# One scan of logarithms in place of two scans of products, in a fused decayed attention and feed-forward kernel

## The chip, the cores and the metric

One NeuronCore of a Trainium2 chip runs the whole program. The metric is device time in microseconds (us). Names: TensorE is PE (its weight loads are PEld), VectorE is DVE, ScalarE is ACT, GpSimd is POOL, and SP is the queue that issues nearly all DMAs.

## The reference

Four batches of eight heads, 768 steps, head size 48. Each step multiplies a 48 x 48 complex state by a complex decay per row, adds the outer product of k and v to its real part, and reads it with q. The result feeds a feed-forward layer (384 to 2048 to 384) with g = h * sigmoid(1.702 h).

```python
mag = np.sqrt(a_re * a_re + a_im * a_im)
scale = np.minimum(mag, 0.999) / (mag + 1e-06)
a_re_n, a_im_n = (a_re * scale, a_im * scale)
...
for t in range(S):
    ar, ai = (a_re_n[:, :, t, :, None], a_im_n[:, :, t, :, None])
    new_re = ar * S_re - ai * S_im
    new_im = ar * S_im + ai * S_re
    kv = np.einsum('bhd,bhe->bhde', k[:, :, t], v[:, :, t])
    S_re, S_im = (new_re + kv, new_im)
    y[:, :, t] = np.einsum('bhd,bhde->bhe', q[:, :, t], S_re)
```

The inputs: a_re is uniform in 0.85 to 0.95, a_im is normal with a spread of 0.1.

## The kernel before

The 4 x 768 steps are twelve units of 256 steps (`prepare(u)`, `attend(u)`); the first unit is prepared in two halves of 128. A unit is prepared in the layout rows x steps, three groups of rows side by side (NR = 3), so that 256 steps are tiles of 128 x 768 elements, and a half is 128 x 384.

`prepare_part` turns the decays into factors. Per step it needs the magnitude min(mag, 0.999) / (1 + 1e-6 / mag) and the angle of the complex number. Squares of re and im (`sqr`, `sqi`) are added (`sum`); Ln and Exp with scale 0.5 give mag (`root`); the angle is twice arctan(im / (re + mag)), with a maximum-and-add on DVE (`den`), a reciprocal by Ln and Exp (`logd`), a product (`ratio`) and Arctan (`atan`). A second reciprocal (`logc`) and a line on it (`w`) make the small correction. A backward scan of products (`sp`) gives the decay from each step to the end of the unit, which scales k; a forward scan of products (`qm`) that starts at the reciprocal of the unit's whole decay (`edge`) gives its inverse, which scales q. A third scan sums angles (`theta`); rounding, absolute value and two Sin give cosine and sine, with which q and k are turned. Ten DMAs per unit (`remap`; for halves too) bring q and k to the layout of heads x steps.

`attend` multiplies q and k to scores (p_ps), masks them on DVE (pm), multiplies them and the running state with v (x_ps), copies the result as x, and updates the state (kz_ps, st). `moe(n)` takes blocks of one or two units through the hidden layer (h_ps, Silu on ACT) and the output layer (o_ps). The weights come as 64-bit words and are made into fp32 on ACT and DVE (`convert`); from the third block on they are split in two parts (`split`), three matmuls each. `inspect`, `sign` and `decide` look at the inputs' ranges; if one is out of bounds a slow general branch runs. `clear` zeroes the tile qkh1 in pieces on POOL.

ACT's functions stand in table sets: LOGS (Ln, Exp), TRIG (Arctan, and Sin for the first unit), SILU (Silu, Sin). Where the next activation needs another set, a table load is put ahead of it.

All this is recorded as operations in a `Plan`; a stored order (`ORDER`, a packed list of numbers) says in which order they are issued, and `OTHER` names those that run in their second form on another engine. Each engine takes its instructions strictly in that order.

Of the kernel before, what the change touches and what calls it, by code (L numbers as in the profile page):

```python
# [106 lines left out]
}  # L107
ORDER = (
    "08jve0000A00jUK0A&DD08s!_0D}O808{{l0962n09F8p09OEr09gP509XKB0E++v0Eqw#09pWF09yc$00sbz0FVG&0A2u!0AT=)0AK)-0Am1-"
    "0Ac|U0FwZ}00#hQ0I2|y0G9w{0BHaM0BQgX0A~PZ0Bitj0F(f20Ga^^0B!*Z0F?l50SW+{0B``70C50w0TBS40GR-u0CE8m0G$930CWJK0D%CQ"  # L110
    "0H6R30CfQq0CoVP0Tcjt0HFY*0C)fr01*JB0HpyH00aQC0T}?Q0Hy&J0H*+X0Sf@L0JH!I0D1uz0H^?~0JQ)K0T=+b0IUHT022Uv0IdMH0DJ)-"
    "02u&%03!f?0Ji}k01g1I02BbP0J#8v0k#1f0Vn{v03HCq0J{O00I&eO0KovU0Vx2z0Kx#i0LTEt0K@>v0UZFv0V)8-0UiMi0UQ7%0LlQz0Du7@"
    "03`s_0VM#-0NMa10V4q`0U`hz0M!5|0M-B-02Kf?0N?-|02Tox0N4QB0k{Cy0L%a#0W1K{0NDT+0k;4x03QI)0O9}`0NVf{03iS<0WJX00Ve?A"
    "0MP+003rb105|~S05SmG0l5I*0VV;u0WbjP0lNV&0WkpN0lxvf0WtvQ0W$%;0L=lw05bsX04V{!04@M30PFxO05t&80W<*a0ObHI0W|>V0Sy5*"
    "051SK0O|ng05AYK0mA_605JgX05k!`0P+FB05$<Q0mcEs0S*B306YQ20Mh}-06_po0Pq3M0m%Um0YL#d0YU*o0Pz7j0Ym}M0XG4r0Y?Bk0XqQo"
    "0X+f8080Tp0Yw4J0QdpQ0Z0M<0Zjo(0Qmqt0Y(5m0nh<H0ZIWs06zfq0Qvy?06+mw0iXd(073!M0agG<0QLb_0Z#x!07L;$07wB$07U^<0YCuv"
    "0a*Y^0hRzv0RI8e07?K&0Z{<{0RaF`0n`D^0n-5d0nGvc0o4Hg0sjHk0RRC~0s#S20oMW80a^f00aOA40ipq10s{d80bK!A0t5mG0bT)O0ha;>"
    "0onoy0cipU0oeiD0b>FV0o(y!0uKRb0tEqO0v7=T0crvY0dE2f0;U050b~LV0t*5d0uTXo0R#aB0c!zn0R{pR0ucff0uuq>0bl{>0rUaj0cHW-"
    "0vQ1Z0cQcS0viEg0qFv#0ki>Z0jdFU0vZCX0pS650;mD%0pbC50vrOV0v!St0c`<r0;&Ps0dfKB0hs}$0eS+f0v`dI0u=#s0w4mg0v-YG0qg>?"
    "0;~cd0rdgz0ek`D0ptR-0p$Vk0rmlV0h|Hx0wV!<0eu3p0qp`L0<{7n0p<aQ0<!^k0h<Ay0wn?R0jvVJ0rvu~0f7OX0=fZt0p|j*0rLT{0fzyf"  # L120
    "0=5Bw0=WYF0=EJ90e%7|0j>hS0=xl(0x$w60r>*J0x<#l0=ohG0x|+T0sH}f0fGX-0{j7l0sR8Q0w@AA0{sDn0>lFX0jL5g0f_;K0yF|D0yY9G"
    "0yhFZ0{#Ll0xbcd0yqLL0gVFx0zLvY0yzRd0xtoh0y+Xl0?z{g0g3{?0y_f*0=)r?0|o-e0gM7i0zd(e0>}c!0!RWu0|5fb0geJf0!acx0>T1H"
    "0z?8#0>uH40!0E#0|NsG0#gFZ0i^>30|^3B0#^dc0}2BO0?Y#q0?h(V0g(d_0!{&v0$l=F0}cZV0#pJ|0#ySH0h0rm0$c)F0h9t(0$~Fb0$KwR"
    "0$u@?0jC2M0?-2x0#E|k0$Ty80$&3b0%ihY0$>7B0?q<t0%!vh0~i8h1DXR80%rpm0@?!61DOLC0~-Qm0&4@C0~!My0%-%B0^0&?0&xQ!0^9>0"
    "0jmOP1DyhG0@MQ110VyU0^I?v0^b861ET_N0^kFr0^S3j1Em6R1EvDg1E&KY0&fGV0&)W)0(AqR0j~n#1FQn(1D^ub0^$PJ0&@c60_6hN0`CK%"
    "0(%1R1E>Pn1E~V>1FiwF0(t^=10(|E0(1iB0(b)Q0(=5@1F-`20_XyL1F{110_g(k0)GLs0_y_y0_*{`10@1}273bc1FHgs1MCAP0{8>70__5M"
    "27Cjw0`vp011AE20{H_d11<uD27LoB27Uti1FZsr0)YeV1Fr+M0)qqY0)_*(27dyF0*M1K0*(TT12G1G1GWN)27v?f13Cha1Gxf=1G)l?27&^U"
    "0`3Fv10w_Q0+|E21Mvg91NH;*12h9E12O|D12Y3V12qHp11kcM12zLJ0*wQ_0+9nZ0+Ivt0+<6W13U(U0+a@X12_Y{0-6Iq1Hc140+j-m13m-#"
    "1NZ|u1Nj5{1HJ;61HS^B0-XY!13&_v1O5X+0-ysz1N8$#1ONh`14IM-289Hb1N{U428IHm14agi1O)^F14RO&1O@`514jc+14#o)14{;o15W~^"
    "14ssm1P2C+1Hl7R1OWre15g7@1Iq*i15E=_1PKI}1Iz<i1HuE%1eOE{15yTy15^f#16T%)0;L1i1JDD`1H%K+16l)C1H=Rh1egR1162f>17ZVP"  # L130
    "1Pum`1P%lP1eycV16KoF1JeV~17rq|1Plg{17HJP1P=pV178E+1Jnb>29X2T1K|Xp1e^oL1IGlL1L6Z?17!rD1P}w`29g8F17QRa29pD417-vg"
    "1QP?;18f7;1fv9@1f&F_1g8Vp18xK41f2us18M_k1gQp;1IYxQ19k&%1Lp>n1KI|b1f>IQ18D@_1f~OU1giwD19$`#18W0u1g`_=19t=E19AiD"
    "19JqZ2A2bL2ABk@2AKpO1KR|!1m6S}19=171hNC_1Kk8519}7@2ATta1M37A1R?~p2Ac%n2Al(X19b!51gr$%1hE7o1mXjH1Q-UL1A+u41g!&p"
    "1APXb1SSNu1QZ6J1hxZ#1S<oB1K$MY1SbQ31BC;G1SkaK1Q`Ui1R4Y+1S|%i1n30h1RDe#2B8Gz1iA*I1SteH1RVsv1i1r<1iJ+11ndMh1iS?4"
    "1T6!K2BQOp1S$j`1UCdO1ULhX1UUpR1TX~Z1Th5e1TqBc1nmQj1UmzV1B(PY1C9oy1n>r>1BnBV1oQ+v1TzHh1T+Nl1h)jZ1Cj%f1Ca#x1Cs>t"
    "1%?Dd1C#{w1VIEw1C<2$1o;F#1WW`&1VjUt1Vsc(2Bri@1V{w+1W5!<1oi~`1XTq51WpF01&9Wy1U>{$1iu9S1V04G1o{Nj1pfs61WE&!1Xl$B"
    "1px(z1W*Nu1XBc21&Ri#1X2WF1p@@h1&aj01q1{@1ib{o2C4+g1&ju(1XcuC1&##*1&{<;1XKkD1j__r1YHDL1&;(<1i}Q)1k41(1kD7*1&svH"
    "1l0sw1jPhm1(pQR1jYnl1knV?1(5}m1(yb_1(gMo1YQQM1(OAs2Cf8T1Zf1;1)2q)1la`F1Z4!$1Y-pd1ZoDa1ZxGE2CxMY1lR_#1ZD-C1ZM=("
    "1qKD11rh{v2C@Yc2D1gA2DAmC1=|E@1Z)MP1Z@SR1r`Mq1a1V{2DJqj1)c=k1)T*41snw21sDW%2DSur1aAcy2Db&=1r-Ev1)>F}1aSm-1*Zk2"
# [878 lines left out]
```

## Time and profile before

| | |
|---|---|
| median of 3 runs | 564.99 us (564.89 to 565.46) |
| profiled execution, first to last instruction (span) | 563.2 us |
| PE busy | 532.4 us, 95% |
| PE weight loads | 442.2 us, 79% |
| DVE busy | 447.3 us, 79% |
| ACT busy | 313.2 us, 56%, of it 61 table loads with 78.3 us |
| POOL busy | 24.5 us, 4% |
| granted TensorE clock | 1.00 throughout |

The profile gives no time of that execution but its span; the median of the runs is some 1.8 us longer. PE starts late and is then busy to the end: its row in 40 slices of 14 us reads 0, 2, 8 and then 9 to the last. DVE and ACT are most taken in the first third.

### The profile page before, as it was taken

The page shows a single profiled execution, that of the slowest core. Times are in us where ns is not written, and L with a number is a line of the kernel's source. Part 1 is how long each engine was busy: PE and PEld are TensorE (multiplying, and loading weights), DVE is VectorE, ACT ScalarE, POOL GpSimd, SP SyncE. Part 2 cuts the span into 40 slices and gives each one's busy share as a digit, 9 for nine tenths or more (in the row PEclk, how much of TensorE's full clock was granted, in tenths as well). Part 3 has the DMA queues.
Part 4 walks back from the last instruction along what each step waited for, and adds up shares of the span by engine and source line. Part 5 has one row for each costly group of instructions (what it writes and reads, how often), then busy time and mean ns, then how long its engine had stood idle before and what let it go on. Part 6 is the DMA issues. An engine that isn't in the chain of part 4 may idle for free.

```text
span 563.2 us, 14767 instructions
## 1 busy us (share of the span) xinstructions
PE 532.4 (95%) x6236; PEld 442.2 (79%) x6236; DVE 447.3 (79%) x820; ACT 313.2 (56%) x460; POOL 24.5 (4%) x86
## 2 busy tenths in 40 slices
...
GB/s 307 199 194 359 181 381 76 222 102 221 72 146 119 128 148 101 113 150 122 136 180 75 167 128 210 45 227 94 103 138 56 203 122 87 51 52 70 29 61 110
DMA packets 30902, 80.06 MB, mean 142 GB/s; under 512 B 4208, under 2 KB 7024, under 8 KB 30832
## 3 DMA queue, kind: packets, MB, share of 16 engines
...
HBM read 55.44 MB, written 4.72 MB: 107 GB/s over the span
## 4 chain that ended last, share of the span: by engine, by line
PE 92%; DVE 5%; ACT 1%; DMA 1%; issue 0%; DVEq 0%
PE o_ps L646 37%; PE h_ps L613 37%; PE x_ps L532 7%; PE p_ps L507 5%; PE kz_ps L563 4%; PE kz_ps L557 3%; DVE s L427 1%; DVE qk L271 1%; DMA ri<-in_a_dram 1%; DVE pm L511 1%; DVE s L271 0%; DVE qr L271 0%; DVE s L409 0%; DVE s L393 0%; DVE valA L298 0%
## 5 line engine op out<-in xcount | busy, mean ns | idle before, releaser
L626 ACT ACTIVATE g<-h_ps 128x512 f32<-128x512 f32 x80 | 46.3, 596 | 120.8 <-PE h_ps L613 79.7
L613 PE MATMUL h_ps<-xhi,hiA 128*128 128x512 f32 x240 | 95.9, 400 | 0.0
L646 PE MATMUL o_ps<-gh,hiU 128*128 128x512 f32 x240 | 95.5, 398 | 0.0
L646 PE MATMUL o_ps<-gl,hiU 128*128 128x512 f32 x240 | 93.7, 390 | 0.0
L613 PE MATMUL h_ps<-xhi,loA 128*128 128x512 f32 x240 | 93.6, 390 | 0.0
L646 PE MATMUL o_ps<-gh,loU 128*128 128x512 f32 x240 | 93.5, 390 | 0.0
L613 PE MATMUL h_ps<-xlo,hiA 128*128 128x512 f32 x240 | 93.5, 389 | 0.0
L843 ACT ACT_TABLE_LOAD x61 | 78.3, 1283 | 1.9 <-PEq L1006 0.8
L630 DVE CAST gh<-g 128x512 fp32r<-128x512 f32 x70 | 29.4, 421 | 42.5 <-PE o_ps L646 25.5
L632 DVE TENSOR_TENSOR gl<-g,gh 128x512 fp32r<-128x512 f32 x80 | 54.5, 684 | 3.0 <-ACT gh L629 1.3
L646 PEld LDWEIGHTS o_ps<-gl,hiU 128*128 128x128 f32 x240 | 45.0, 188 | 10.0 <-DVE gl L632 0.4
L613 PEld LDWEIGHTS h_ps<-xhi,loA 128*128 128x128 f32 x240 | 45.0, 188 | 9.6
L680 DVE TENSOR_REDUCE fit<-raw_w 128x1 f32<-128x256 f32 x96 | 38.1, 413 | 18.0 <-DMA raw_w<-in_w_out_dram 17.7
L646 PEld LDWEIGHTS o_ps<-gh,hiU 128*128 128x128 f32 x240 | 45.1, 188 | 9.2 <-issue 0.4
L646 PEld LDWEIGHTS o_ps<-gh,loU 128*128 128x128 f32 x240 | 45.1, 188 | 8.7
L613 PEld LDWEIGHTS h_ps<-xlo,hiA 128*128 128x128 f32 x240 | 45.1, 188 | 8.5
L613 PEld LDWEIGHTS h_ps<-xhi,hiA 128*128 128x128 f32 x240 | 45.1, 188 | 8.5
L511 DVE TENSOR_TENSOR pm<-p_ps,mask 128x512 f32<-128x512 f32 x48 | 32.8, 682 | 17.2 <-PE p_ps L507 13.9
L566 ACT ACTIVATE kt<-kz_ps 128x224 f32<-128x224 f32 x66 | 23.3, 353 | 40.5 <-PE kz_ps L563 29.9
L271 DVE TENSOR_TENSOR qk<-qk,s 128x768 f32<-128x768 f32 (+1 forms) x52 | 45.7, 889 | 0.0
L646 PE MATMUL o_ps<-g,valU 128*128 128x256 f32 x192 | 45.3, 380 | 0.0
L613 PE MATMUL h_ps<-x,valA 128*128 128x256 f32 x192 | 45.0, 381 | 0.0
...
## 6 DMA issues: line engine op xcount, KB each, us to landing
...
```

What stands on the lines that cost most here:

```text
L271: add(en, t, rank, lambda: e.tensor_tensor(out=out, in0=a, in1=b, op=alu), **kw)
L507: mm(p_ps[to : to + QL, j, lo:L], lhsT=at(h, 1, c)[:, lo : lo + QL], rhs=at(h, 0, c)[:, lo:L], start=True, stop=True)
L511: add("DVE", d_t(CW), rk(4 * c + hh), lambda hh=hh: dve.tensor_tensor(out=pm[hh], in0=p_ps, in1=mask, op=ALU.mult), r=["P"], w=[f"pm{hh}"])
L532: mm(x_ps[32 * j : 32 * j + 32, r, :], lhsT=lt, rhs=rt, start=n == 0, stop=n == len(steps) - 1)
L566: one = ("ACT", a_t(2 * KD) - 0.12, lambda e=e: act(out=kt[0][:, 2 * e : 2 * e + 2, :], in_=k_ps, func=AF.Copy))
L613: mm(h_ps[hb][:, hs], lhsT=ww[:, r * T + f * P : r * T + (f + 1) * P], rhs=x[:, r, :], start=r + k == 0, stop=r == NR - 1 and k == len(ter ...
L626: add("ACT", a_t(N) - 0.15, rk(i + f / 2), lambda hb=hb, hs=hs: act(out=g32[hb][:, hs], in_=h_ps[hb][:, hs], func=AF.Silu, scale=SLOPE), r ...
L630: two = ("DVE", d_t(N, 2), lambda hb=hb, hs=hs: dve.tensor_copy(out=high.g(hb)[:, hs], in_=g32[hb][:, hs]))
L632: add("DVE", d_t(N), rk(i + f / 2), lambda hb=hb, hs=hs: dve.tensor_tensor(out=glo[hb][:, hs], in0=g32[hb][:, hs], in1=high.g(hb)[:, hs].b ...
L646: mm(o_ps[m][:, 0:N], lhsT=y[:, f * DM + m * P : f * DM + (m + 1) * P], rhs=x[:, hs], start=i == 0 and f == 0 and k == 0, stop=i == NP - 1 ...
L680: add("DVE", d_t(CK), rk + 2, lambda x=x, op=op: dve.tensor_reduce(out=f_w[:, x, n : n + 1], in_=weights.looked_at()[:, :, 1], op=op, axis ...
L843: nc.scalar.preload_act_table_set(o[5])
```

## The change

The two scans of products become one backward scan that sums logarithms (ADD of min(0.5 Ln(mag^2), Ln 0.999), SUBTRACT of Ln(1 + 1e-6 / mag)), started at LIFT = 14. ACT takes Exp of it for k, and Exp of its negative for q; the common factor e^14 cancels. The clamp, the reciprocal and the forward scan (`edge`, `scan_qm`) are gone, and so are `root`'s Exp and the DVE line `w`. The angle is arctan(im / re) itself: `den` is gone, and `logd` takes Ln and Exp of re. For that the check of the inputs is another: re must be at least |im| (`extent` in place of `sign`, with twice the loads and reduces), and late units get a reduce of |im| beside that of re. The turn in `theta` is 2 pi, not pi. The order and the list of second forms are new.

```diff
-        square("sqi", u, i, rk("sqi"), d, i_, r=ks("im"), w=k_den, tab=opening)
-        both("sum", u, i, rk("sum"), m, m, d, ALU.add, r=k_den, w=k_mag)
+        square("sqi", u, i, rk("sqi"), c, i_, r=ks("im"), w=k_rec, tab=opening)
+        both("sum", u, i, rk("sum"), m, m, c, ALU.add, r=k_rec, w=k_mag)
+        add("ACT", a_t(C), rk("logd"), lambda: act(out=d, in_=r_, func=AF.Ln, bias=b_tiny), r=ks("re"), w=k_den, tab=LOGS, grp=u or None)
+        add("ACT", a_t(C) - 0.1, rk("logd"), lambda: act(out=d, in_=d, func=AF.Exp, scale=-1.0), w=k_den, tab=LOGS, grp=u or None)
         add("ACT", a_t(C), rk("root"), lambda: act(out=m, in_=m, func=AF.Ln, bias=b_tiny), w=k_mag, tab=LOGS, grp=u or None)
-        add("ACT", a_t(C) - 0.1, rk("root"), lambda: act(out=m, in_=m, func=AF.Exp, scale=0.5), w=k_mag, tab=LOGS, grp=u or None)
-        add("DVE", d_t(C) + 0.18 * C / (NR * T), rk("den"), lambda: dve.scalar_tensor_tensor(
-            out=d, in0=r_, scalar=0.0, in1=m, op0=ALU.max, op1=ALU.add
-        ), r=ks("re") + k_mag, w=k_den)
...
+            add("DVE", d_t(NR * T), rk("low"), lambda: dve.tensor_reduce(
+                out=f_i[:, u - LATE : u - LATE + 1], in_=i_, op=ALU.max, axis=AX.XY, apply_absolute_value=True
+            ), r=["im.0", "im.1"], w=["fi"])
+        add("ACT", a_t(C) - 0.1, rk("logc"), lambda: act(out=c, in_=m, func=AF.Exp, scale=-0.5), r=k_mag, w=k_rec, tab=LOGS, grp=u or None)
+        add("ACT", a_t(C), rk("logc"), lambda: act(out=c, in_=c, func=AF.Ln, scale=1e-6, bias=ones), w=k_rec, tab=LOGS, grp=u or None)
...
         add("DVE", w_t(C), rk("z"), lambda: dve.tensor_scalar(
-            out=m, in0=m, scalar1=0.999, scalar2=None, op0=ALU.min
+            out=m, in0=m, scalar1=0.5, scalar2=LOG_MAX, op0=ALU.mult, op1=ALU.min
         ), w=k_mag)
...
-                    initial=1.0, op0=ALU.mult, op1=ALU.mult,
+                    initial=LIFT, op0=ALU.add, op1=ALU.subtract,
...
-        def edge():
-            dve.tensor_scalar(out=rc, in0=w(sp)[:, :, 0], scalar1=A_MIN, scalar2=None, op0=ALU.max)
-            dve.reciprocal(out=rc, in_=rc)
...
-        add("DVE", NR * (s_t(n) + 0.055), rk("qm"), scan_qm, r=k_mag + k_rec + [f"rc{u % 2}"], w=k_qm)
+        add("ACT", a_t(C) - 0.1, rk("qm"), lambda: act(out=w(qm), in_=w(sp, 1, 1), func=AF.Exp, scale=-1.0), r=k_sp, w=k_qm, tab=LOGS, grp=u or None)
+        add("ACT", a_t(C) - 0.1, rk("sp"), lambda: act(out=w(sp, 0, 1), in_=w(sp, 0, 1), func=AF.Exp), w=k_sp, tab=LOGS, grp=u or None)
+        add("POOL", 0.13, rk("qm"), lambda: pool.tensor_scalar(
+            out=fa, in0=w(sp)[:, :, 0], scalar1=math.exp(-LIFT), scalar2=None, op0=ALU.mult
+        ), r=k_sp, w=[f"fa{u}.{i}"])
...
-        add("POOL", 0.45, 14 + 0.5 * n, lambda: pool.memset(part, 0.0), r=["rc0"], w=[f"H1.{c}.{x}" for c in range(2) for x in range(2)])
+        add("POOL", 0.45, 14 + 0.5 * n, lambda: pool.memset(part, 0.0), r=["s3.0"], w=[f"H1.{c}.{x}" for c in range(2) for x in range(2)])
```

The first place where the order differs is POOL at the program's start, behind the masks. In the rows, s is a tile of the preparation, fit the table of checks, qkh_76 the tile that is zeroed in pieces. Before:

```order
L386 MEMSET s_80 128x3
L382 MEMSET s_82 128x3
L386 MEMSET s_80 128x3
L405 COPY fit<-s_83 128x3
L382 MEMSET s_82 128x3
L721 MEMSET qkh_76 128x513 x2
L405 COPY fit<-s_83 128x3
L721 MEMSET qkh_76 128x513
L458 COPY qr<-fit 128x3
L458 COPY qk<-fit 128x3
L721 MEMSET qkh_76 128x513
L386 MEMSET s_82 128x3
```

And of the change:

```order
L385 MEMSET s_82 128x3
L389 MEMSET s_80 128x3
L385 MEMSET s_82 128x3
L715 MEMSET qkh_76 128x513
L389 MEMSET s_80 128x3
L715 MEMSET qkh_76 128x513 x2
L404 TENSOR_SCALAR fit<-s_83 128x3
L715 MEMSET qkh_76 128x513 x5
L404 TENSOR_SCALAR fit<-s_83 128x3
L450 COPY qr<-fit 128x3
L450 COPY qk<-fit 128x3
```

Three pieces of zeroing now stand ahead of the first copy of the edge (L404, which waits for the decay's Exp), and five in a row behind it; before they were spread over the opening and beyond it.

The second place is DVE in the opening, where the decay's scans of the second half and the angles stand; s_83 is the sum or product of decays, s_85 the angle. Before:

```order
L393 SCALAR_TENSOR_TENSOR s_83<-s_80,s_82 128x129 x3
L271 TENSOR_TENSOR s_81<-ri,s_81 128x3x128
L401 TENSOR_SCALAR small<-s_83 128x3
L402 RECIPROCAL small<-small 128x3
L393 SCALAR_TENSOR_TENSOR s_83<-s_80,s_82 128x129 x3
L427 SCALAR_TENSOR_TENSOR s_85<-small,s_81 128x128 x3
L409 SCALAR_TENSOR_TENSOR s_84<-s_80,small,s_82 128x128 x3
L437 SCALAR_TENSOR_TENSOR s_85<-s_85,s_81 128x3x128
L271 TENSOR_TENSOR qk<-qk,s_83 128x3x128
L271 TENSOR_TENSOR qk<-qk,s_84 128x3x128
L440 TENSOR_SCALAR small<-s_85 128x3
```

And of the change:

```order
L429 SCALAR_TENSOR_TENSOR s_85<-s_85,s_81 128x3x128
L277 TENSOR_TENSOR s_81<-ri,s_81 128x3x128
L436 SCALAR_TENSOR_TENSOR s_80<-s_85 128x3x128
L277 TENSOR_TENSOR qk<-qk,s_84 128x3x128
L386 TENSOR_SCALAR s_80<-s_80 128x3x128
L277 TENSOR_TENSOR qk<-qk,s_83 128x3x128
L432 TENSOR_SCALAR small<-s_85 128x3
L396 SCALAR_TENSOR_TENSOR s_83<-s_80,s_82 128x129 x3
L277 TENSOR_TENSOR qr<-qk,s_80 128x3x128 x2
L419 SCALAR_TENSOR_TENSOR s_85<-small,s_81 128x128 x3
```

The clamp (L401), the reciprocal (L402) and the scans of L409 have gone; two tensor-scalar instructions, L386 (halving and minimum) and L432 (the angle's carry), stand around the second product.

The third place is ACT ahead of the copies of x, from the rounding of the second half's angle (L434 before, L426 now) on. Before:

```order
L434 ACTIVATE s_81<-s_85 128x3x128
L254 ACTIVATE s_82<-ri 128x3x256
L443 ACTIVATE s_80<-s_85 128x3x128
L254 ACTIVATE s_81<-ri 128x3x256
L446 ACTIVATE s_80<-s_80,small 128x3x128
L447 ACTIVATE s_85<-s_85 128x3x128
L843 ACT_TABLE_LOAD
L368 ACTIVATE s_82<-s_82,small 128x3x256
L294 ACTIVATE valA_238<-raw_74 128x768
L369 ACTIVATE s_82<-s_82 128x3x256
```

And of the change, the first rows from one Sin on:

```order
L439 ACTIVATE s_85<-s_85 128x3x128
L837 ACT_TABLE_LOAD
L402 ACTIVATE s_84<-s_83 128x3x128
L426 ACTIVATE s_81<-s_85 128x3x128
L403 ACTIVATE s_83<-s_83 128x387
L837 ACT_TABLE_LOAD
L438 ACTIVATE s_80<-s_80,small 128x3x128
L300 ACTIVATE valU_150<-raw_73 128x768
L300 ACTIVATE valA_166<-raw_74 128x768
L439 ACTIVATE s_85<-s_85 128x3x128
L260 ACTIVATE s_82<-ri 128x3x256
L837 ACT_TABLE_LOAD
```

Before, one table load stands between the second half's rounding and the logarithms of the next unit (L368; L373 of the change). Now two stand there, and a third just ahead of the rounding, since the two Exp of the decay's sum come between one Sin and the next.

## Rows read from the trace of the kernel before

**Rows 1.** The page: busy time and share of each engine; the chain that ended last, by engine.

```profile
PE 532.4 (95%) x6236; PEld 442.2 (79%) x6236; DVE 447.3 (79%) x820; ACT 313.2 (56%) x460; POOL 24.5 (4%) x86
...
PE 92%; DVE 5%; ACT 1%; DMA 1%; issue 0%; DVEq 0%
```

**Rows 2.** Windows: stretch, its length, each engine's busy time (instructions); clock, DMA share, GB/s.

```profile
0.00:43.63 43.63, 17.02 (x326) 13.02 (x327) 39.81 (x82) 34.28 (x56) 9.99 (x30) 1.00 0.68 239
43.63:100.00 56.37, 56.37 (x645) 48.55 (x645) 55.46 (x90) 51.39 (x75) 4.04 (x11) 1.00 0.77 242
100.00:460.00 360.00, 359.90 (x4456) 299.43 (x4455) 305.49 (x545) 211.73 (x300) 10.44 (x45) 1.00 0.53 137
460.00:563.23 103.23, 99.13 (x813) 81.24 (x812) 46.51 (x106) 15.81 (x31) 0.00 (x0) 1.00 0.21 66
...
151.40:233.80 82.40, 82.35 (x1071) 68.63 (x1064) 72.88 (x125) 58.18 (x79) 3.00 (x13) 1.00 0.51 126
```

**Rows 3.** Waits of PE: line waited for, us in total, times, longest.

```profile
PE h_ps L454 <- DVE small L440: 24.6, 1, 24.6
```

**Rows 4.** Timeline before the first hidden matmul: start, length, engine, line, operation.

```profile
40.74 0.69 DVE L511 TENSOR_TENSOR pm<-p_ps,mask 128x512 f32<-128x512 f32 x1 [0.25 <-PE p_ps L507]
...
43.07 0.49 ACT L542 ACTIVATE x<-x_ps 128x384 f32<-128x384 f32 x1 [1.68 <-PE x_ps L532]
...
43.63 1.11 PE L613 MATMUL h_ps<-x,valA 128*128 128x256 f32 x4
```

**Rows 5.** Groups of DVE instructions up to 43.8 us: busy us, mean ns of one.

```profile
L271 DVE TENSOR_TENSOR qk<-qk,s 128x384 f32<-128x384 f32 x8 | 4.3, 549 | 0.0
...
L409 DVE TENSOR_TENSOR_SCAN s<-s,small,s 128x128 f32<-128x128 f32 x6 | 2.4, 460 | 0.0
...
L427 DVE TENSOR_TENSOR_SCAN s<-small,s 128x256 f32<-128x256 f32 x3 | 2.0, 749 | 0.0
...
L401 DVE TENSOR_SCALAR small<-s 128x3 f32<-128x3 f32 x2 | 1.3, 650 | 0.0
L370 DVE SCALAR_TENSOR_TENSOR s<-ri,s 128x384 f32<-128x384 f32 x2 | 1.1, 560 | 0.8 <-ACT s L369 0.8
...
L370 DVE SCALAR_TENSOR_TENSOR s<-ri,s 128x768 f32<-128x768 f32 x1 | 1.0, 953 | 0.0
```

**Rows 6.** Timeline of ACT in the opening.

```profile
25.81 1.28 ACT L843 ACT_TABLE_LOAD   x1
27.10 0.94 ACT L368 ACTIVATE s<-s,small 128x768 f32<-128x768 f32 x1
27.94 1.09 ACT L294 ACTIVATE valA<-raw 128x768 uint16<-128x768 uint32 x1
28.89 0.81 ACT L369 ACTIVATE s<-s 128x768 f32<-128x768 f32 x1
...
31.94 0.34 ACT L566 ACTIVATE kt<-kz_ps 128x224 f32<-128x224 f32 x1
32.18 0.84 ACT L378 ACTIVATE s<-s 128x768 f32<-128x768 f32 x1
32.92 0.83 ACT L380 ACTIVATE s<-s 128x768 f32<-128x768 f32 x1
```

**Rows 7.** Timeline of DVE and POOL where one stands beside the other.

```profile
13.09 1.14 DVE L401 TENSOR_SCALAR small<-s 128x3 f32<-128x3 f32 x1
...
13.22 0.98 POOL L721 MEMSET qkh<- 128x513 f32 x2
...
18.97 0.16 DVE L401 TENSOR_SCALAR small<-s 128x3 f32<-128x3 f32 x1
...
30.98 1.01 DVE L295 TENSOR_SCALAR raw<-raw 128x768 int32<-128x768 int32 x1
...
31.05 0.52 POOL L721 MEMSET qkh<- 128x513 f32 x1
```

**Rows 8.** Timeline of ACT at the end.

```profile
559.05 0.60 ACT L661 ACTIVATE o<-o_ps 128x512 f32<-128x512 f32 x1 [6.16 <-PE o_ps L646]
```

More of the change, by code (lines that the diff above doesn't have):

```diff
@@ L114 @@
[L114 to L118, printed above, removed]
@@ L433, in prepare_part @@
         add("DVE", NR * (s_t(n) + (0.0 if first else 0.055)), rk("theta"), theta, r=k_den + ([] if first else [f"cr{c0}"]), w=k_th)
-        one = ("ACT", a_t(C) - 0.1, lambda: act(out=nn_, in_=t, func=AF.Copy, scale=1.0 / math.pi))
-        two = ("DVE", w_t(C), lambda: dve.tensor_scalar(out=nn_, in0=t, scalar1=1.0 / math.pi, scalar2=None, op0=ALU.mult))
+        one = ("ACT", a_t(C) - 0.1, lambda: act(out=nn_, in_=t, func=AF.Copy, scale=1.0 / TURN))
+        two = ("DVE", w_t(C), lambda: dve.tensor_scalar(out=nn_, in0=t, scalar1=1.0 / TURN, scalar2=None, op0=ALU.mult))
         either(on("turns", u, i), one, two, rk("theta"), r=k_th, w=k_den)
         add("DVE", d_t(C), rk("theta"), lambda: dve.scalar_tensor_tensor(
-            out=t, in0=t, scalar=1.0 / math.pi, in1=nn_, op0=ALU.mult, op1=ALU.subtract
+            out=t, in0=t, scalar=1.0 / TURN, in1=nn_, op0=ALU.mult, op1=ALU.subtract
         ), r=k_den, w=k_th)
         add("DVE", 0.07, rk("theta"), lambda: dve.tensor_scalar(
-            out=crs[c1], in0=t[:, :, n - 1], scalar1=math.pi, scalar2=None, op0=ALU.mult
+            out=crs[c1], in0=t[:, :, n - 1], scalar1=TURN, scalar2=None, op0=ALU.mult
         ), r=k_th, w=[f"cr{c1}"])
```

145 lines of the change are left out of this document (70 added, 75 removed), and 10 rows, old and new, of the table OTHER.

## Prediction

> **What bounds the kernel now.** I read the page's busy shares first, then the chain that ended last, the windows, and TensorE's waits. TensorE (PE) is busy 95% of the span, and 92% of the chain is its own matmuls [rows 1]. The windows say where the missing part lies: up to 43.63 us PE is busy 17.02 us, from there to 460 us its idle time is 0.10 us in all, and the 4 us that it lacks in the last window are the tail after its last matmul [rows 2]. Its list of waits agrees: one of 24.6 us before its first instruction [rows 3]. So from 43.63 us, when the first hidden-layer matmul of the feed-forward part starts [rows 4], the kernel is a fixed amount of PE work in a row. VectorE (DVE) is 79% busy, and a faster DVE is worth nothing there. What can move is (a) the moment of that first matmul, (b) new stalls behind it, (c) the tail.
>
> The span is 563.23 us; the median of the runs is 564.99, 1.76 above it. I make the sum on the span and carry the 1.76 unchanged.
>
> **The change, part by part.** *What sets 43.63 us.* The last steps are DVE's product of scores and mask (40.74 us), the matmuls on it, ScalarE's (ACT's) copy of x (43.07 us), and the first hidden matmul 0.56 us after that [rows 4]. From the product's start to the copy's are 2.33 us. DVE is busy 39.81 of the 43.63 us before, ACT 34.28 [rows 2], so both lists count.
>
> *DVE ahead of that last product.* Gone: the six short second scans (2.4 us), the clamp of the edge (1.3) with its reciprocal, and the maximum-and-add (two of 0.56, one of 0.95) [rows 5]; and the order now puts the long angle scan of the second unit (2.0 us) behind the product, not ahead of it. Together 7.8 us. New ahead of it: one rounding and two absolute values of 384 columns (0.5 each) that were ACT's, and one copy of 224 columns (0.4): 1.9 us. Net 5.9 us less DVE work.
>
> *ACT ahead of the copy.* The order shows nine table loads where there were four: the chunks of the first unit now pass Ln and Exp, Arctan, Exp and Sin in turn. A load is 1.28 us, and the next activation starts as it ends (25.81 + 1.28 against 27.10) [rows 6]; five more cost 6.4 us.
>
> The Trainium skill, page "ScalarE: Activation LUTs", section "What ACT_TABLE_LOAD costs", gives 1.28 us for the load and a drain of 1.38 us besides, 2.66 us per switch. The trace doesn't show the drain. By that page's price the five loads would cost 13.3 us, and the change would lose at once.
>
> *Where ACT becomes the chain.* From the rounding of the second half's angle to the last copy of x, ACT's list now holds 25 instructions. By their steps from start to start [rows 6]: four loads of 1.28 make 5.1; five activations of 768 columns without a bias, 0.74 (32.18 to 32.92), 3.7; two Ln, 0.84 (27.10 to 27.94), 1.7; four conversions of weights, 0.95 (27.94 to 28.89), 3.8; five copies of 224 columns, 0.24 (31.94 to 32.18), 1.2; four of 384 columns at 0.5, 2.0; one copy of x, 0.4. Sum 17.9 us. That part starts when DVE's angle scan of the second half ends.
>
> *When that scan ends.* ACT starts at 4.1 us as before, when the first input lands. Ten activations of 384 columns at 0.48 (half of the 768-column steps, and 0.1) bring 8.9 us, a load 10.2, Arctan 10.7, a load 12.0, six more 14.9: then the first Exp of the decay is done. GpSimd (POOL), which waits for it, copies the edge and does five pieces of zeroing in a row, where the old order spread them. A piece is 0.49 us (two in 0.98) [rows 7]: POOL is taken from about 15.2 to 17.6. On DVE the thirteen rows from the first weight's mask to the product with the scale take 7.0 us: three of 768 and six of 384 columns at 0.47 (printed 0.55 [rows 5], less the 0.08 by which neighbours overlap), two short ones at 0.34, six scans at 0.34. The first of them is held by three more zeroing pieces, which run right behind POOL's masks to 8.0. So DVE comes to its next tensor-scalar instruction at 15 to 15.2.
>
> Such instructions don't run beside zeroing: the clamp of three columns at 13.09 took 1.14 us, to the end of two pieces on POOL that started at 13.22, and the same clamp at 18.97 took 0.16; at 30.98 a shift took 1.01, beside a piece at 31.05 [rows 7]. The Trainium skill, page "SBUF — State Buffer", section "Who interferes with whom", says that VectorE's fast modes and GpSimd share a port pair as a lock, and that the loser waits for the whole instruction; the trace agrees, and adds that two pieces in a row were both waited for.
>
> So one of two tensor-scalar instructions there (the halving with a minimum, or the three-column carry) waits for 17.6. From there: 0.3, one product 0.5, the carry 0.1, three scans 1.0, two products 0.9, the angle's three scans 1.2: 21.6 us, or 20.8 if it is the carry that waits. I take 21.2. With ACT's 17.9 the copy of x starts at 39.1. DVE's list behind the scan is 16.1 us (ten of 384 and five of 768 columns at 0.47, four sums of 0.88, two of 0.87, four masked products of 0.6, three copies of 0.3, the decay 0.5): its last product starts at 36.7, and by it the copy at 39.0 too. Since two chains meet there I add 0.5: copy at 39.6, first hidden matmul at **40.2 instead of 43.63, 3.4 us earlier**. If nothing waits for POOL, the scan ends at 19.4 and the matmul is at 38.3, 5.3 us earlier; if the waits of today, in which ACT stood idle 9.35 of 43.63 us [rows 2], come back beside the five loads, it is near 43.
>
> *Behind it.* PE's list has the same matmuls; one transposing pair and one set of state matmuls, some 0.6 us together, now stand ahead of the first hidden one. Against that the order changes between kinds of matmul more or less tightly: I take 0, with 1 us to either side. New on DVE are the largest |im| of nine units (a reduce of 768 columns each) and ten more reduces with their ten loads for the first three units; each unit loses a scan, a maximum-and-add and two short ones. DVE had 0.91 us idle from 43.63 to 100 us [rows 2] and gets more. In the tail nothing moves: the last matmul, a copy of 0.60 us on ACT [rows 8], the last DMA; the verdict on the inputs is now reached earlier on DVE, ahead of five more differences.
>
> Sum: 563.23 - 3.4 + 0 = 559.8 of span, with 1.76 **561.6 us**.
>
> **The rivals.** *No wait for POOL.* If the zeroing meets scans and two-input products alone, the opening gains 5.3: 559.7 us. For it: only two of the old order's pieces in the opening cost anything. Against it: now five stand in a row, and two tensor-scalar instructions fall into their 2.4 us.
>
> *The opening stays.* ACT is the chain, and its five loads take what DVE gives up: 564 to 565 us. For it: 25 instructions without a gap, in which any late input counts. Against it: ACT idled 9.35 us there.
>
> *ACT becomes the bound of the third block (slower).* Between the last Silu of the second block and that of the third the old order gives ACT 77 instructions with 13 loads, and it is busy 58.18 of 82.40 us [rows 2]. The new order has 110 there, with 22 loads: nine loads of 1.28 are 11.5 us, and 24 activations at some 0.65 (splits of 512 columns and units prepared earlier) 15.6. That is 85.3 us for 82.4. If PE needs all of it, it waits 3 us and, with the waits inside, some 6 on top of the forecast: 567.6 us. It decides when the stall passes 4.5 us. Against it: the stretches before and behind hold fewer, so part of the 24 is work done early, for which nobody waits yet; and PE showed no stall at ACT's 51.39 of 56.37 us from 43.63 to 100 [rows 2]. By the Trainium skill's 2.66 us per switch (the page and section above) those nine loads would be 23.9 us, the stretch 98 us of ACT's work, and the kernel some 15 us slower. I give that price 0.03 of this case's 0.15, since the rows show the next activation right behind a load [rows 6].
>
> *The check fails and the general branch runs*: many times slower. The inputs' re is at least 0.85 and im has a spread of 0.1, so I give it nothing.
>
> **How the numbers follow.** Forecast (3.4 us, give or take 1.7) 0.46; no wait for POOL 0.19; opening stays 0.20; ACT bound 0.15. What a measurement here can tell from no change is 0.2%, 1.1 us. Faster by more takes the first two, a third of the third and a fifth of the fourth: 0.75. Within: 0.14. Slower: 0.11. The range reaches from the second case with 1 us of regrouping, 558.4, to just above the third, 565.6; the forecast's own is 559.9 to 563.3.
>
> **What would show it.** First hidden matmul at 39 to 42 us, PE without idle from there; a tensor-scalar instruction of DVE stretched to about 2 us between 15 and 17.6 us, beside five zeroing pieces; nine table loads before the copy of x, each 1.28 us with the next activation right behind; ACT over 90% busy in the third block, and PE still without waits. Wrong would be: waits of PE for ACT's Silu or copies between 140 and 235 us; a last copy of x that waits for PE while ACT idles; a load followed by idle time.

## The result and the profile after

The changed kernel takes 570.86 us (median of four runs, 568.1 to 572.86) against 565.0 before: a ratio of 1.0094, 95% interval 1.0073 to 1.0114. It is slower by 0.9%, where 0.6% faster was forecast, and outside the range of 558.4 to 565.6. Its times also spread over 5 us, where those of before lie within 0.6. One of the kernel before's 24 executions beside the last runs below took 1102 us and is left out of the ratios.

The profiled execution is one of the shorter ones: a span of 566.4 us, 1.7 below its own time of 568.1, as before. Its span is 3.2 us longer than that of before, and this splits into three parts:

| | before | after | difference |
|---|---|---|---|
| start to first hidden matmul | 43.63 us | 41.01 us | -2.62 |
| from there to the start of the last output matmul | 514.99 | 519.32 | +4.33 |
| from there to the end (tail) | 4.61 | 6.07 | +1.46 |

The page of the changed kernel, busy time of each engine and the instruction queues (packets, MB, share of 16 engines):

```profile
PE 534.5 (94%) x6236; PEld 447.1 (79%) x6236; DVE 404.9 (71%) x726; ACT 358.2 (63%) x507; POOL 26.0 (5%) x86
...
q8 instruction: 49, 0.80, 0.6%
q14 instruction: 21, 0.17, 0.1%
```

DVE has 42 us less to do and ACT 45 more, as the change intends. The windows, with the same columns as in [rows 2]:

```profile
0.00:41.01 41.01, 18.18 (x361) 14.26 (x361) 34.77 (x71) 36.27 (x54) 12.00 (x32) 1.00 0.73 257
41.01:100.00 58.99, 56.97 (x618) 48.90 (x612) 53.17 (x84) 55.04 (x76) 3.92 (x12) 1.00 0.77 230
100.00:140.00 40.00, 39.42 (x516) 34.21 (x518) 39.31 (x60) 36.73 (x54) 2.86 (x9) 1.00 0.69 177
140.00:220.00 80.00, 80.00 (x1089) 67.12 (x1081) 76.83 (x129) 69.82 (x95) 2.84 (x12) 1.00 0.63 163
220.00:240.00 20.00, 19.13 (x347) 16.23 (x346) 18.37 (x34) 19.06 (x23) 0.65 (x4) 1.00 0.86 199
240.00:460.00 220.00, 220.00 (x2401) 183.54 (x2403) 143.91 (x272) 119.77 (x170) 3.77 (x19) 1.00 0.51 130
```

PE was dense from 43.63 us on before [rows 2]. Now it idles 2.02 us between 41 and 100 us, 0.58 by 140 us, and 0.87 between 220 and 240. In the third block (140 to 220 us), where the slower rival put ACT's wait, it idles 0.00. Its list of waits says what ended them:

```profile
PE h_ps L446 <- DVE qk L277: 21.0, 1, 21.0
PE kz_ps L549 <- issue: 1.5, 2, 0.9
PE p_ps L499 <- issue: 1.0, 1, 1.0
PE kz_ps L555 <- DVE st L564: 0.7, 1, 0.7
...
PE h_ps L605 <- issue: 0.6, 1, 0.6
...
PE h_ps L605 <- ACT g L614: 0.3, 1, 0.3
```

"issue" is the new word here: [rows 3] had none behind the opening. Four waits, 3.1 us in this list, were ended by nothing that the profile shows. They stand in the middle of groups of equal matmuls, as in this timeline of PE ahead of the first hidden matmul:

```profile
39.65 0.44 PE L549 MATMUL kz_ps<-v,kt 128*32 128x48 f32 x18
40.72 0.36 PE L549 MATMUL kz_ps<-v,kt 128*32 128x48 f32 x14 [0.63 <-issue]
41.01 0.48 PE L605 MATMUL h_ps<-x,valA 128*128 128x256 f32 x1
```

Eighteen matmuls of the state run, then PE idles for 0.63 us (0.83 from the start of the eighteenth to that of the next), then the other fourteen run. The profile shows no operand that comes late in the middle of such a group. I counted PE's instructions (matmuls, weight loads and 65 records of its sequencer) in the trace: ahead of the four waits stand 705, 1473, 2753 and 5569 of them (the instructions are called by these numbers below). Each is 193 more than a multiple of 256. The trace also has the packets of queue q8: 49 of 16,384 bytes, about one for each 256 of PE's 12,537 records. So the theory for what follows is **instruction fetch**: PE's list comes in blocks of 256, the packet of a block is asked for near the time at which the block ahead of it is entered, and if that block passes quickly, or the packet is held up, PE stands. The rival is that the new order itself makes PE wait, for data or for ACT's table loads.

What the records of PE and of q8 give for single blocks (us; "entered" is the first instruction of the block ahead, "wanted" is when the last one of it starts):

```
kernel    instruction  entered  packet from, to   wanted   came
before        1473       76.02   77.59   78.61     81.64   81.65
after          705       34.89   38.53   39.51     39.88   40.72
after         1473       79.74   81.81   82.85     82.95   84.23
after         2753      129.39  131.46  132.90    133.23  134.18
after         5569      221.83  224.73  226.31    226.90  227.97
```

The instruction comes 1.2 to 1.7 us after its packet has ended. The kernel before shows no such wait: none of its blocks behind the opening passes in under 4.9 us, though it too has stretches in which 256 instructions pass in 2.6 us. They lie across two blocks.

### The profile page after: what moved, and what is told of

The parts are those of the page before. It is cut to its first block, busy times and chain, and to the rows that moved or that the text cites. A ratio compares the mean times of both kernels' runs of the same rounds, so it can differ in the third digit from the quotient of the medians.

```text
span 566.4 us, 14721 instructions
## 1 busy us (share of the span) xinstructions
PE 534.5 (94%) x6236; PEld 447.1 (79%) x6236; DVE 404.9 (71%) x726; ACT 358.2 (63%) x507; POOL 26.0 (5%) x86
## 4 chain that ended last, share of the span: by engine, by line
PE 89%; DVE 5%; ACT 2%; issue 2%; DMA 1%; SPq 0%; POOL 0%; ACTq 0%; DVEq 0%
PE o_ps L638 36%; PE h_ps L605 35%; PE x_ps L524 7%; PE p_ps L499 5%; PE kz_ps L555 3%; PE kz_ps L549 3%; DMA raw<-in_w_out_dram 1%; DVE qk L277 1%; DVE s L419 1%; DVE s L277 1%; ACT L837 1%; ACT valA L300 0%; DVE qr L277 0%; DVE pm L503 0%; DVE valA L304 0%
## 5 line engine op out<-in xcount | busy, mean ns | idle before, releaser
L621 ACT ACTIVATE gh<-g 128x512 fp32r<-128x512 f32 x45 | 28.3, 629 | 41.7 <-PE o_ps L638 41.4
L672 DVE TENSOR_REDUCE fit<-raw_w 128x1 f32<-128x256 f32 x96 | 36.5, 413 | 10.9 <-DMA raw_w<-in_w_out_dram 8.1
L605 PEld LDWEIGHTS h_ps<-x,valA 128*128 128x128 f32 x192 | 35.7, 190 | 7.0 <-issue 1.2
```

Source lines behind the costliest of these rows:

```text
L605: mm(h_ps[hb][:, hs], lhsT=ww[:, r * T + f * P : r * T + (f + 1) * P], rhs=x[:, r, :], start=r + k == 0, stop=r == NR - 1 and k == len(ter ...
L621: one = ("ACT", a_t(N) - 0.1, lambda hb=hb, hs=hs: act(out=high.g(hb)[:, hs], in_=g32[hb][:, hs], func=AF.Copy))
L672: add("DVE", d_t(CK), rk + 2, lambda x=x, op=op: dve.tensor_reduce(out=f_w[:, x, n : n + 1], in_=weights.looked_at()[:, :, 1], op=op, axis ...
```

## The experiments

The kernel before took 565.6 to 565.8 us in these comparisons (564.9 beside the two single executions). Expectations are quoted as they stood before each run.

### The changed kernel again (a_same, a_same2, a_same3)

No edit.

> The changed kernel as it is, for a second trace of it. Theory (instruction fetch): TensorE stops where the next 256 of its instructions are not there yet, so the waits that the profile puts down to nothing stand again ahead of the same instructions (number 705, 1473, 2753 and 5569 of its list, the 193rd of a block of 256), with other lengths, since they hang on when a 16 KB packet of the instruction queue gets through: 2 to 6 us in all behind 25 us. The times spread over some us, 568 to 573. Rival (the order's own waits): the same waits with the same lengths to 0.1 us, as waits for other engines have, and then the spread of the times is left without a cause.

Measured: 570.87 us (567.36 to 574.95, six runs). The traced execution took 570.21 us. The four waits stand ahead of the same four instructions; from start to start they last 0.83, 2.16, 0.91 and 1.28 us (0.83, 1.28, 0.96, 1.07 in the first trace). The positions are fixed and the lengths are not, as the fetch theory says. The waits for ACT and DVE near 55, 74 and 77 us lasted 0.47, 0.65 and 0.74 (0.46, 0.64, 0.85). This trace also shows what made this execution longer. Its windows behind the wait of 2.16 us, columns as above:

```profile
82.00:84.00 2.00, 0.55 (x20) 0.28 (x8) 1.85 (x4) 2.00 (x5) 0.00 (x0) 1.00 0.26 90
84.00:86.00 2.00, 1.56 (x31) 1.42 (x32) 0.69 (x1) 1.98 (x3) 0.60 (x3) 0.92 0.04 11
86.00:88.00 2.00, 2.00 (x10) 1.29 (x12) 0.07 (x1) 0.71 (x2) 0.00 (x0) 0.50 0.00 0
88.00:90.00 2.00, 2.00 (x81) 1.88 (x78) 1.88 (x3) 0.00 (x0) 0.00 (x0) 0.72 0.00 0
```

PE was busy 0.55 of 2 us, and then the granted clock fell from 1.00 to 0.50 (1.2 instead of 2.4 GHz) for 3.4 us; its matmuls of 256 columns start 0.43 us apart there instead of 0.23. The wait cost 2 us and the clock 1.7 more.

> The changed kernel again, for a trace of one of its longer executions. Theory: an execution beyond 570 us holds one of TensorE's waits for its instructions, at the same places (705th, 1473rd, 2753rd, 5569th), of 2 us or more, and behind it the granted clock falls to half for 3.4 us, as in the trace of 570.2 us; one below 569 us holds four waits of 0.7 to 1.5 us and no stretch at half clock behind 30 us and ahead of TensorE's end. Rival: the longer executions spread their loss over many places.

> As the run above, one more trace of the changed kernel, with the same expectation.

Measured: 568.22 and 568.35 us. The expectation was half wrong. Both traces show the wait at the 1473rd instruction with 2.16 and 2.21 us, without a fall of the clock ahead of PE's end. So not each wait of 2 us lowers the clock, and it is the clock that marks the execution of 570 us. The granted clocks of the ten executions in the two comparisons agree: the seven of 570 us and more have a mean of 0.992 to 0.996, the three below 569 one of 0.998 or 0.999. In the first of the two the wait at the 705th instruction is missing, in the second that at the 5569th.

### The same program, its blocks shifted (a_pad44, b_pad18)

```diff
     nc.vector.memset(p_ps, 0.0)
+    for _ in range(44):   # 18 in the kernel before
+        nc.tensor.matmul(h_ps[0][0:1, 0:1], lhsT=ones, rhs=ones, start=True, stop=True)
```

> The changed kernel with 44 matmuls of one column (176 instructions) ahead of everything on TensorE, where it idles till 21 us; nothing else differs. Theory (instruction fetch): the bounds of the blocks of 256 instructions move by 176, away from the stretches in which 256 instructions pass in 3 us; the four waits (0.8, 1.3, 0.7, 1.1 us) go, up to 1.3 us of others come, and the first hidden matmul starts near 40.2 us instead of 41.0. The three waits near 55.5, 74.2 and 77.1 us (1.4 us in all) stay, since ACT and DVE cause them. Time 564 to 566 us, and less spread. Rival (the new order itself makes TensorE wait, for data or on its queue): moving the instructions changes nothing, 568 to 573.

Measured: 567.35 us (565.43 to 569.63, twelve runs), ratio to before 1.0030, interval 1.0017 to 1.0043. That is 3.5 us less than the changed kernel beside it, for 176 instructions added ahead of everything. All four waits are gone, and the first hidden matmul starts at 40.16 us. The waits near 55, 74 and 77 us stayed. A new one came at the 3009th instruction, again 193 more than a multiple of 256, in a block that takes 5.3 us without it; its packet ran from 132.52 to 133.55 us, 4.25 us after the block ahead was entered. PE's timeline there:

```profile
133.01 0.76 PE L501 MATMUL p_ps<-qkh 128*32 128x128 f32 x31
135.13 0.19 PE L501 MATMUL p_ps<-qkh 128*32 128x32 f32 x1 [1.36 <-issue]
```

Thirty-one matmuls of a group of 32 run, and the last one stands 1.36 us for its instruction. The time missed the expected 566 by 1.4 us.

The two traced executions lie closer together than the medians: 567.84 us here and 568.1 for the changed kernel, with 519.3 us from the first hidden to the last output matmul in both. The three waits that are gone behind the first hidden matmul give back 3.0 us, counted from start to start against the same matmuls. The new wait takes 1.5 of it again, and another 1.3 go where PE, now earlier, has to wait for DVE and ACT:

```profile
230.75 0.41 PE L557 MATMUL kz_ps<-ident,qkh 112*128 112x112 f32 x2 [0.32 <-DVE st L566]
...
261.57 0.41 PE L557 MATMUL kz_ps<-ident,qkh 112*128 112x112 f32 x2 [0.49 <-ACT kt L560]
```

So the run shows what the four waits hang on. Why the medians lie 3.5 us apart these two traces don't show.

> The kernel before with 18 matmuls of one column (72 instructions) ahead of everything on TensorE, in its idle opening. Theory (instruction fetch): now blocks of 256 instructions end inside its dense stretches (near 295, 316, 356 and 481 us a block would pass in 2.9 to 3.3 us), so waits that the profile puts down to nothing appear there, 0.3 to 1.3 us each; time 566 to 569 us and a wider spread. Rival: 565.0 as without them.

Measured: 567.56 us (567.3 to 567.93), ratio 1.0035, interval 1.0022 to 1.0048. An addition that computes nothing makes the kernel before 1.9 us slower. But not by the waits that were expected: the fast blocks near 295, 316, 356 and 481 us passed in 2.9 to 4.3 us without any. Their packets came 0.9 to 2.6 us before the block ahead was even entered. The loss lies in the opening: the first hidden matmul starts at 45.92 us instead of 43.63. Of these 2.3 us 0.7 stand in the trace at 12 us already, where a conversion on DVE starts at 11.94 us instead of 11.21, before PE's first transposing matmul; the rest comes with one wait at the 705th instruction:

```profile
43.12 0.39 PE L534 MATMUL x_ps<-pm,v 128*32 128x128 f32 x4
44.66 0.30 PE L534 MATMUL x_ps<-pm,v 128*32 128x128 f32 x2 [1.15 <-issue]
```

So a fast block alone doesn't make a wait; its packet has to be late too. I took all traces of this study together, and of the blocks behind 45 us those whose packet started after the block ahead was entered; for each I took the share of the 16 DMA engines that the data queue held from half a microsecond before that entry until the packet. Where that share was under a quarter (159 blocks), the packet started 1.5 us after the entry at the latest. Where it was 0.95 or more (106 blocks), 63 started later than 2 us, the last at 4.9. All 32 waits of this kind of 0.5 us and more, those of the opening included, came with a share of 0.87 or more.

### Two loads issued later (a_late)

```diff
+    for n, after in ((447, 307), (747, 536)):   # qk behind a product; re and im behind v
+        order.remove(n); order.insert(order.index(after) + 1, n)
...
+            if n == 447:
+                dma(out=spare, in_=pm[1][0:1, 0, 0:1])
             o[3]()
```

> The changed kernel with two loads issued later and nothing else moved: the 768 KB of q and k that SP issues at 77.07 us are held until DVE's product at 80.7 us (by a DMA of one number that reads that product), and the 768 KB of re and im issued at 128.74 us go behind the load of v at 131.40. Both are wanted 10 us later. Theory (instruction fetch, late because the data queue is full): the data queue runs dry about 80.5 us instead of 82.4, the packet of instructions gets through by 81 us instead of 81.8 to 82.85, and the wait ahead of the 1473rd instruction (1.3 us, 2.2 in the second trace) falls below 0.3; that ahead of the 2753rd (0.9) falls below 0.4; those of the 705th and the 5569th stay. 568 to 569.5 us. Rival (the fetch is late because of TensorE's own pace, whatever else moves): both waits stay within 0.3 us of 1.3 and 0.9.

This tests the cause and not only the place. The same stretch of the changed kernel and of this one; the share of the data transfers is the last column but one. The changed kernel:

```profile
79.00:80.00 1.00, 1.00 (x21) 0.76 (x23) 0.45 (x2) 1.00 (x2) 0.00 (x0) 1.00 0.99 392
80.00:81.00 1.00, 0.98 (x46) 0.72 (x34) 1.00 (x3) 1.00 (x2) 0.10 (x1) 1.00 1.03 390
81.00:82.00 1.00, 1.00 (x54) 0.86 (x57) 0.86 (x2) 1.00 (x3) 0.11 (x1) 1.00 1.08 393
82.00:83.00 1.00, 1.00 (x44) 0.96 (x32) 1.00 (x3) 1.00 (x3) 0.00 (x0) 1.00 0.37 135
83.00:84.00 1.00, 0.23 (x8) 0.00 (x0) 1.00 (x3) 1.00 (x3) 0.00 (x0) 1.00 0.00 0
```

And with the loads later:

```profile
79.00:80.00 1.00, 1.00 (x46) 0.86 (x48) 0.68 (x2) 1.00 (x3) 0.00 (x0) 1.00 0.51 186
80.00:81.00 1.00, 1.00 (x46) 0.61 (x39) 0.90 (x3) 1.00 (x3) 0.20 (x2) 1.00 0.01 3
81.00:82.00 1.00, 1.00 (x60) 1.00 (x51) 0.96 (x2) 1.00 (x2) 0.01 (x1) 1.00 0.00 0
82.00:83.00 1.00, 1.00 (x54) 0.99 (x44) 1.00 (x3) 1.00 (x3) 0.00 (x0) 1.00 0.00 0
```

There PE's packet started at 81.81 us, just as the data queue began to run dry, and PE stood from 82.95 to 84.23. Here the packet starts at 79.45 us, 0.13 after the block ahead was entered; that block passes in 3.07 us, and PE doesn't wait. The second load was moved too little: its wait stayed (0.87 us), since the packet of that block still started 2.05 us late. The time didn't follow: 571.49 us (566.92 to 573.54, four runs), 1.0116, where 568 to 569.5 was expected. The traced execution is that of 566.92 us, with waits of 1.38 and 1.78 us at the 705th and 5569th instruction and a mean granted clock of 0.998. What the three longer ones hold isn't in a trace; their mean clock is 0.993 to 0.995.

### Which part the lists of ACT and DVE have (a_pad49_moved)

```diff
+    for n, after in ((62, 239), (64, 432), (452, 205), (453, 452)):
+        order.remove(n); order.insert(order.index(after) + 1, n)
```

and 49 matmuls ahead, as above. Operation 239 is the Silu that PE waited for at 74.2 us, 62 a conversion on ACT that stood in front of it, 64 that conversion's DVE half; 205 is the state's sum, 452 and 453 two lines on the angle.

> The changed kernel with 49 matmuls of one column ahead of everything on TensorE (196 instructions; of all shifts the one that leaves the fewest fast blocks), and four operations moved by a few places: the Silu that TensorE waited for at 74.2 us ahead of a conversion of weights on ACT (with its table load), that conversion's DVE half one place later, and the state's sum that TensorE waited for at 77.1 us ahead of two lines on the angle on DVE. Theory (instruction fetch, and ACT and DVE lists for the rest): the wait at 74.2 us (0.4) goes, that at 77.1 us (0.7) falls to 0.2, and of the fetch's waits at most 1.5 us are left; 565 to 566.5 us. Rival (the waits hang on the table loads as such): moving the Silu moves its load along, and the wait stays; 566.5 to 568, as with 44.

Measured: 567.59 us (565.59 to 569.76), which misses the 565 to 566.5 expected and is no gain on 567.35 with 44. The wait for the Silu goes, as the theory says, though the Silu takes its table load along; so the rival's reason fails. But a new one stands near the same place, for the state's sum on DVE: 0.79 us from start to start, where the Silu's was 0.65 with 44. In the changed kernel and here:

```profile
74.47 0.70 PE L605 MATMUL h_ps<-x,valA 128*128 128x256 f32 x2 [0.26 <-ACT g L614]
...
71.68 2.32 PE L607 MATMUL h_ps<-x,valA 128*128 128x256 f32 x10
74.41 0.53 PE L551 MATMUL kz_ps<-v,kt 128*32 128x48 f32 x32 [0.41 <-DVE st L566]
```

The wait near 77 us shrank from 0.85 to 0.60, and 0.57 came back at 79 us. Such moves pass the loss on; 1.4 us of waits belong to the new order's lists.

### The tail (a_tail6, a_noim, b_dma10, a_oneload)

At the end SP waits for each of eight DMA semaphores in turn, and the DMAs take these in rotation. With the ten added loads the last output counts on the first of the eight, before it was the seventh. Besides, SP of the changed kernel pauses 0.8 us fifteen instructions behind its last branch. Four kernels:

```diff
+                for x in range(6):    # a_tail6, and range(10) in b_dma10 (kernel before)
+                    dma(out=spare[0:1, x : x + 1], in_=nat[0][0, x : x + 1, 0:1])
```

```diff
-  rk, lambda ...: dma(out=half(), in_=a_in[u, :, lo:hi]),                   # 20 loads
+  rk, (lambda: None) if y else lambda ...: dma(out=half(), in_=a_in[u, :, lo:hi]),   # a_noim: no |im|
+  rk, (lambda: None) if y else look,      # a_oneload: ten loads of re and im side by side
```

> The changed kernel with six DMAs of one number each behind the last load that looks at the weights, so that the last output's DMA counts on the same semaphore (the seventh of eight) as in the kernel before; in the changed kernel it is the first of the eight, on which SP waits at the end before it looks at the other seven. Theory (tail): the stretch from the start of TensorE's last instruction (L710) to the end of the span falls from 5.75 us by 0.6, or to 4.3 us as before if SP's pause of 0.8 us inside it goes as well; the time falls by as much. Rival (the last output lands later by itself): the tail stays at 5.7 us.

> The kernel before with ten DMAs of one number each behind the last load that looks at the weights, as many as the change adds. Theory (tail by SP's list): the last output counts on the first of the eight semaphores and SP pauses once more, as in the changed kernel; the stretch from the start of the last output matmul to the end grows from 4.6 to 6.0 us, and the time from 565.6 to 567. Nothing else changes: TensorE is without waits behind 43.6 us. Rival: tail and time stay (within 0.2 us).

> The changed kernel without the ten loads and reduces of |im| of the first three units that the new check of the inputs added (a zero stands in their place, so that part of the check is left out). Theory (tail by SP's list): SP's list is as long as before, the last output counts on the seventh semaphore again, and the stretch from the start of the last output matmul to the end falls from 6.1 to 4.6 us; with it the time by 1.4 us, to 569. Rival A (the tail is longer because of something else in the new program): 6.0 us still. Rival B (the loads delay TensorE's instruction packets): the waits at the 1473rd, 2753rd and 5569th instruction fall below 0.5 us; the looks start behind 100 us, so the first of them can't change by that.

> The changed kernel with re and im of the first three units looked at by ten loads instead of twenty: each brings both, and the two reduces read its two halves. All that the kernel checks is still checked. SP's list is as long as before. Theory (tail by SP's list): the stretch from the start of the last output matmul to the end is 4.6 to 4.9 us instead of 6.1, and the time falls by 1.2 us, to 569.5. Rival (in the run without the loads of |im| the tail was short because the reduces were gone too): 6 us.

| | instructions of SP | semaphore of the last output | tail | time |
|---|---|---|---|---|
| before | 431 | seventh | 4.61 us | 565.0 us (565.6 to 565.8 beside those below) |
| b_dma10 | 441 | first | 5.17 | 566.24 (1.0009, 0.9996 to 1.0023) |
| after | 463 | first | 6.07 | 570.86 |
| a_tail6 | 470 | seventh | 5.99 | 570.66 |
| a_noim | 445 | seventh | 4.91 | 567.13 |
| a_oneload | 445 | seventh | 4.94 | 567.23 (1.0033, 1.0018 to 1.0048) |

In b_dma10 the place of the semaphore comes to 0.5 us of the tail's 0.56, since the last output landed 0.1 us later after its issue as well (1.4 was expected, and the time's difference is unclear). By SP's records the changed kernel's 1.46 us are 0.2 of later landing, 0.5 of the place and 0.8 of the pause. Putting it back in the changed kernel gained nothing, as the pause grew to 1.2 us: that expectation fell. The pause is there in all traces with 463 to 470 instructions on SP (0.55 to 1.2 us) and missing in all with 431 to 446, and with the ten loads joined into the others the tail is 4.9 us. The trace has four packets of 8 KB on the other instruction queue right behind the branch (563.07 to 563.69 us in the changed kernel); that SP's pause is such a fetch was only argued.

The times of the last two fell by 3.6 us and not by 1.2. Their traces show waits as in the changed kernel at the 1473rd, 2753rd and 5569th instruction (1.25, 1.81 and 1.51 us in a_noim, 0.78, 0.96 and 1.16 with the loads joined), so 2.4 us of it stay open. A guess is that fewer of their executions meet the clock's fall: the mean granted clock of their runs is 0.996 to 1.000, that of the changed kernel's ten 0.992 to 0.999.

### What can be had together (a_best)

The edits of a_late and a_oneload with 49 matmuls ahead.

> The changed kernel with both edits above and 49 matmuls of one column ahead on TensorE. Theory: first hidden matmul at 39.6 us (43.6 before), from there to the last output matmul 516.5 us (515.0 before; 1.4 us of waits for ACT and DVE near 55, 74 and 77 us stay), tail 4.9: span 561, time 562.7 us, 0.5% faster than the kernel before. If the fetch finds other fast blocks under a full queue: up to 565.

Measured: 564.61 us (563.1 to 566.38, twelve runs), ratio to before 0.9984, interval 0.9970 to 0.9999. It is 6 us faster than the changed kernel and level with the one before: 0.16% is less than the 0.2% that the prediction called the least to be told from no change. The 562.7 us expected were missed; the 565 named for the case that the fetch finds other fast blocks were kept. Start to first hidden matmul 39.21 us, from there to the last output matmul 517.48, tail 5.24; two waits for instructions are left (0.70 at 133 us, 0.68 at 226 us). With the shift and the loads the change's gain of 4.4 us in the opening is nearly paid for by 2.5 behind it and 0.6 in the tail; 1.3 of span remain (561.9 for 563.2 us).

## Why the prediction was wrong

The forecast's span of 559.8 us became 566.4 in the trace: 0.8 of the difference lie in the opening, 4.3 behind it and 1.5 in the tail. The median lies another 2.8 us above the traced execution.

**The opening: right, in part by luck.** "The first hidden matmul 40.2 instead of 43.63" came out at 41.01, of which 0.8 is the wait for instructions shown above; seven other traces of the changed kernel and of those with edits behind the opening have 40.2 to 41.3. The copy of x started at 39.47 us (39.6 forecast). But two steps behind this were off and cancelled. The waits for POOL were put at 2 us. The row is:

```profile
15.58 0.55 DVE L386 TENSOR_SCALAR s<-s 128x384 f32<-128x384 f32 x1
...
16.51 0.44 DVE L432 TENSOR_SCALAR small<-s 128x3 f32<-128x3 f32 x1
...
23.91 0.16 DVE L432 TENSOR_SCALAR small<-s 128x3 f32<-128x3 f32 x1
```

while POOL zeroed:

```profile
15.33 2.56 POOL L715 MEMSET qkh<- 128x513 f32 x5
```

Both tensor-scalar instructions fell into the five pieces, and the short one took 0.28 us more than outside. With pieces of 0.51 us its end, 16.95, is that of the piece that ran (16.87), not that of the last (17.89). By "Who interferes with whom" of the Trainium skill's page "SBUF — State Buffer" the loser waits for the whole instruction; that agrees with one piece. That "two pieces in a row were both waited for" was read from a single row of [rows 7] and doesn't hold in general. The angle's scan so ended at 19.8 us, not 21.2, and ACT's list from there to the copy took 19.6 us, not 17.9, with 1.0 us of waits for PE and DVE inside: no gap had been allowed for.

**"Behind it ... I take 0, with 1 us to either side": the step that failed.** It is +4.3 us in the trace. Of this 1.4 are waits between 55 and 78 us and not in the third block: 0.65 for ACT's Silu, at two places, and 0.75 for the state's sum on DVE. The slower rival had the engine right for the first part and the place wrong, and with PE idle 0.00 from 140 to 220 us ACT's 110 rows there cost nothing. The other 3 us are the three waits for PE's instructions behind the first hidden matmul (1.28, 0.96 and 1.07 from start to start; the fourth lies in the opening), for which no rival stood. The prediction counted the kinds of matmul in each stretch and took their order as free. The order was free for the array, since the waits make up all of the 4.3 us, and not for the list: attention's matmuls come in groups in which 256 instructions pass in 3 us, and where they lie against the blocks and the loads decides.

**"In the tail nothing moves": +1.46 us.** The matmuls and copies are as before; the ten loads turned the semaphores and lengthened SP's list. Why a longer list brings the pause stays open.

**What makes the median 2.8 us longer than the profiled execution** is known in part. In one trace it is the clock: a wait of 2.2 us, and 3.4 us at half the granted clock behind it, which cost 1.7; all executions of the changed kernel of 570 us and more have the lower mean clock. The sum assumed a clock of 1.00. What else makes times of up to 575 us stays open.

**ACT's loads: right.** Nine before the last copy of x, each 1.28 us, and the next activation right behind:

```profile
8.71 1.28 ACT L837 ACT_TABLE_LOAD   x1
10.01 0.53 ACT L391 ACTIVATE s<-s 128x384 f32<-128x384 f32 x1
10.55 1.28 ACT L837 ACT_TABLE_LOAD   x1
11.84 0.62 ACT L375 ACTIVATE s<-s,small 128x384 f32<-128x384 f32 x1
```

Of the chances, 0.11 stood on slower, and none of it on waits for instructions. The lower end of the range is mis-added: the second case with 1 us of regrouping is 558.7, not 558.4, which changes nothing here.
